# Batch 0's attention steps reordered by arrival of the data: keys' transposes ahead of q's, reciprocals split around the exponentials

## The chip, the cores and the metric

The kernel runs on one core of a Trainium2 chip. The metric is the device time of one launch in microseconds (us), lower is better. Two kernels are compared by runs in the same rounds on the same chip. A "look" below is the profiled execution of a kernel.

## The reference, cut to what matters

Attention with keys and values projected from 1024 positions to 64, then a two-layer network on the result. 8 batches, 8 heads, head size 64; the first product of the network is 512 to 2048 columns, the second 2048 to 512.

```python
def _attn_ref(q, k, v, E, F):
    k_proj = np.einsum('ks,bhsd->bhkd', E, k)
    v_proj = np.einsum('ks,bhsd->bhkd', F, v)
    scale = 1.0 / np.sqrt(q.shape[-1])
    scores = scale * np.matmul(q, k_proj.transpose(0, 1, 3, 2))
    scores = scores - np.max(scores, axis=-1, keepdims=True)
    attn = np.exp(scores)
    attn = attn / (np.sum(attn, axis=-1, keepdims=True) + 1e-09)
    return np.matmul(attn, v_proj)

def _moe_ref(x, w_in, w_out):
    h = x @ w_in
    g = h * np.clip(h + 3.0, 0.0, 6.0) / 6.0
    return g @ w_out
```

## The kernel before

The order on each engine is the order of the program (manual schedule). Batch 0 is loaded in pairs of heads, and its attention is worked pair by pair as the loads land; `busy(n)` puts n filler matmuls on constants into TensorE's stream, to keep its clock up while it would wait. All later batches are worked behind the products of the batch before them.

```python
def busy(n):
    ps = pmm()
    for _ in range(n):
        nc.tensor.matmul(ps, ones[:, :P], ones, start=True, stop=True)

for n, j in (("k", 0), ("q", 0), ("v", 0), ("k", 1), ("q", 1), ("k", 2), ("q", 2), ("v", 1),
             ("k", 3), ("q", 3), ("v", 2), ("v", 3)):
    nc.gpsimd.dma_start(out=kqv[0][n][:, 2 * j:2 * j + 2], in_=kqv_dram[n][0][:, 2 * j:2 * j + 2])
# ... w_in, batch 1 and w_out are loaded behind them
# ... E and F are transposed
busy(2)
```

```python
def by_pairs(self):                      # batch 0
    # keys(j): eight matmuls project the keys of pair j, VectorE copies them twice to kp
    # vals(j): the same for the values; the second copy may be later
    keys(0)
    self.q_out(0, self.q_transpose(0, pat))
    self.keys_transposed(0, 2)
    busy(2)
    self.scores(0, pmm)
    busy(3)
    vals(0)()
    keys(1)
    self.q_out(1, self.q_transpose(1, pat))
    lns = logs(0, both)
    self.keys_transposed(2, 2)
    busy(1)
    self.scores(1, pmm)
    recs = inverses(lns)
    av = self.values(0, pat, both)
    busy(3)
    keys(2)
    self.q_out(2, self.q_transpose(2, pat))
    lns = logs(1, one)
    self.keys_transposed(4, 2)
    busy(1)
    out(0, av, recs)
    self.scores(2, pmm)
    recs = inverses(lns)
    vals(1)()
    busy(3)
    keys(3)
    # ... pair 3: q in two halves, one copied by ScalarE; scores 3; values 2; sums 3
    rest.append(vals(3))
    busy(1)
    av = self.values(3, pat, one)
    out(3, av, recs)
    for copy in rest:
        copy()
    busy(4)
# ... then the first product, 16 groups of four matmuls; a group needs all four pairs:
h_ps = pmm()
for ko in range(KO):
    nc.tensor.matmul(h_ps, w_in_sb[:, ko, fo * P:(fo + 1) * P], xT[:, ko, t, :],
                     start=(ko == 0), stop=(ko == KO - 1))
```

The softmax here doesn't subtract the row's maximum and nothing guards it: scores larger than these inputs give would overflow.

## Time and profile before

| | |
|---|---|
| three runs before the prediction | 522.83 to 524.14 us, median 523.99 |
| profiled run | 522.67 us, span on the core 520.9 us |
| first matmul of the first product | 28.11 us |
| last load of batch 0 lands | 22.8 us |
| TensorE busy | 97% of the span |

The lines are shown in the prediction. In the view of the stretches, each row gives the length, then the busy time of each engine with its number of instructions, then the granted clock, the share of the transfer engines and GB/s. In a timeline a row begins with the start and the time to the last end of what it merges; the bracket says how long the engine was idle before and what ended that.

### The profile page before, as it was taken

What the parts mean: (1) busy time and instruction counts of PE and PEld (TensorE: products, weight loads), DVE (VectorE), ACT (ScalarE), POOL (GpSimd) and SP (SyncE); (2) the same over time, 40 slices, a digit from 0 to 9 for tenths busy, and PEclk for the clock granted to TensorE, in tenths of its full rate; (3) what the DMA queues carried; (4) which work ended last, traced back from release to release, by engine and by line L of the source; (5) the groups of instructions that cost most, each with busy time, mean ns of one, the idle gap of its engine ahead of it and who ended that gap; (6) DMA issues with size and microseconds to landing.
All of it is one profiled execution on the core that took longest, in us unless ns stands there. A gap on an engine that the chain in (4) does not pass through costs nothing.

```text
span 520.9 us, 7264 instructions
## 1 busy us (share of the span) xinstructions
PE 506.9 (97%) x2806; PEld 225.1 (43%) x2858; DVE 238.5 (46%) x378; ACT 283.9 (55%) x517; POOL 36.3 (7%) x55
## 2 busy tenths in 40 slices
PE   6899999999999999999999999999999999999996
PEld 3444444444444444444444444444444444444443
DVE  1568636444363453554454354534525544444420
ACT  2677485676446654568437664466635664444431
POOL 7620000100020000200002000200000000000000
PEclk9999999999999999999999999999999999999999
DMA  8999993993049711695119931298111110011112
GB/s 131 203 207 207 207 181 117 190 151 97 22 77 211 145 43 42 117 196 121 42 30 170 176 81 42 63 204 168 42 40 32 40 42 28 34 42 41 40 42 81
DMA packets 67443, 53.95 MB, mean 104 GB/s; under 512 B 29776, under 2 KB 59216, under 8 KB 67408
## 3 DMA queue, kind: packets, MB, share of 16 engines
q0 software_dynamic: 30016, 29.63, 35.6%
q1 hardware_dynamic: 37248, 23.73, 17.3%
q8 instruction: 22, 0.36, 0.3%
q10 hardware_dynamic: 144, 0.13, 0.1%
q14 instruction: 13, 0.11, 0.1%
HBM read 59.24 MB, written 16.78 MB: 146 GB/s over the span
## 4 chain that ended last, share of the span: by engine, by line
PE 94%; DMA 2%; issue 1%; DVE 1%; POOL 1%; ACT 1%; DVEq 0%; ACTq 0%; POOLq 0%
PE mm L393 43%; PE mm L402 41%; PE at L210 3%; PE at L150 3%; DMA q<-in_q_dram 2%; PE at L196 1%; PE mm L84 1%; PE at L180 1%; DVE qTp L187 0%; DVE xT L232 0%; DVE vp L162 0%; PE mm L210 0%; PE mm L196 0%; ACT aT L201 0%; POOL k L95 0%
## 5 line engine op out<-in xcount | busy, mean ns | idle before, releaser
L397 DVE SCALAR_TENSOR_TENSOR g<-r,mm 128x512 bf16<-128x512 f32 x256 | 173.4, 686 | 218.6 <-ACT r L396 218.4
L393 PE MATMUL mm<-xT,w_in_sb 128*128 128x512 bf16 x1000 | 233.1, 380 | 2.6 <-issue 1.9
L402 PE MATMUL mm<-w_out_sb,g 128*128 128x512 bf16 x999 | 230.1, 380 | 1.5 <-issue 0.3
L396 ACT ACTIVATE r<-mm 128x512 f32<-128x512 f32 x256 | 152.3, 603 | 62.6 <-PE mm L393 61.3
L393 PEld LDWEIGHTS <-w_in_sb 128*128 128x128 bf16 x1024 | 96.8, 98 | 125.6 <-issue 14.1
L402 PEld LDWEIGHTS <-g 128*128 128x128 bf16 x1024 | 98.9, 98 | 119.4 <-issue 2.2
L416 ACT COPY o_sb<-mm 128x512 f32<-128x512 f32 x63 | 36.9, 586 | 147.6 <-PE mm L402 144.7
L232 DVE TENSOR_TENSOR xT<-at,rec 128x512 bf16<-128x512 f32 x56 | 38.2, 684 | 16.5 <-ACT rec L228 15.4
L228 ACT ACTIVATE rec<-ln 128x512 f32<-128x512 f32 x64 | 40.4, 640 | 0.1
L223 ACT ACTIVATE ln<-at 128x512 f32<-128x512 f32 x59 | 32.7, 617 | 2.4 <-PE at L210 2.3
L201 ACT ACTIVATE aT<-at 128x512 bf16<-128x512 f32 x56 | 29.2, 612 | 0.9 <-PE at L196 0.9
L358 POOL COPY mark<-kT 1x1 bf16<-1x1 bf16 x5 | 0.9, 177 | 276.4 <-DMA kT<-kp 276.4
L150 PE MATMUL at<-k,ef_t 128*64 128x512 bf16 (+1 forms) x88 | 15.9, 323 | 1.1 <-DMA k<-in_k_dram 1.1
L150 PE MATMUL at<-v,ef_t 128*64 128x512 bf16 (+1 forms) x88 | 15.9, 324 | 0.0
L150 PEld LDWEIGHTS <-ef_t 128*64 128x64 bf16 x176 | 9.6, 109 | 11.4 <-issue 5.9
L162 DVE CAST vp<-at 64x512 bf16<-64x512 f32 (+1 forms) x21 | 11.3, 541 | 4.0 <-PE at L150 3.0
L210 PE MATMUL at<-aT,vp 64*64 64x512 bf16 x112 | 12.3, 379 | 0.5 <-DVE vp L162 0.4
L210 PE MATMUL at<-aT,ones 64*64 64x512 bf16 x118 | 12.7, 400 | 0.0
L84 PE MATMUL mm<-ones 128*128 128x512 bf16 x31 | 10.9, 446 | 1.6 <-DVE ones L77 1.5
L157 DVE CAST kp<-at 64x512 bf16<-64x512 f32 (+1 forms) x21 | 10.2, 522 | 4.3 <-PE at L150 4.3
L210 PEld LDWEIGHTS <-ones 64*64 64x64 bf16 x128 | 3.9, 103 | 13.4 <-issue 13.1
L196 PEld LDWEIGHTS <-kT 64*64 64x64 bf16 x256 | 5.8, 106 | 8.0 <-issue 5.1
(44 smaller groups left out, 94.8 us busy)
## 6 DMA issues: line engine op xcount, KB each, us to landing
out_dram<-o_sb SPq DMA_DIRECT2D x63, 256.0 KB, 2.0
q<-in_q_dram POOLq DMA_DIRECT2D x7, 1024.0 KB, 9.5
k<-in_k_dram POOLq DMA_DIRECT2D x7, 1024.0 KB, 15.0
v<-in_v_dram POOLq DMA_DIRECT2D x7, 1024.0 KB, 19.9
w_out_sb<-in_moe_w_out_dram POOLq DMA_DIRECT2D x4, 512.0 KB, 27.7
w_in_sb<-in_moe_w_in_dram POOLq DMA_DIRECT2D x3, 512.0 KB, 12.6
k<-in_k_dram POOLq DMA_DIRECT2D x4, 256.0 KB, 8.1
q<-in_q_dram POOLq DMA_DIRECT2D x4, 256.0 KB, 8.6
```

The costliest lines, as they stand in the source:

```text
L84: nc.tensor.matmul(ps, ones[:, :P], ones, start=True, stop=True)
L150: nc.tensor.matmul(ps[e * KP:(e + 1) * KP], ef_t[e][:, so, :], kqv[self.b]["kv"[e]][:, hs, so, :], start=(so == 0), stop=(so == SO - 1))
L201: nc.scalar.activation(self.aT[j][:, r].rearrange("p a n -> p (a n)"), tiles[r], AF.Exp, scale=scale)
L210: nc.tensor.matmul(tiles[t][c:c + D].rearrange("p (r n) -> p r n", r=2), stationary(r, 2 * j + a), self.aT[j][r:r + KP, :, a, :], start=Tr ...
L223: nc.scalar.activation(ln, den, AF.Ln)
L228: nc.scalar.activation(rec, ln, AF.Exp, scale=-1.0)
L232: nc.vector.tensor_mul(self.xT[:, j, t, :], av, rec)
L393: nc.tensor.matmul(h_ps, w_in_sb[:, ko, fo * P:(fo + 1) * P], xT[:, ko, t, :], start=(ko == 0), stop=(ko == KO - 1))
L396: nc.scalar.activation(r, h_ps, AF.Relu, bias=0.5, scale=1.0 / 6.0)
L397: nc.vector.scalar_tensor_tensor(g[:, fo, :], r, 1.0, h_ps, op0=ALU.min, op1=ALU.mult)
L402: nc.tensor.matmul(o_ps, g[:, fo, c * P:(c + 1) * P], w_out_sb[:, fo, :], start=(fo == 0), stop=(fo == FO - 1))
L416: nc.scalar.copy(o_sb, o_ps)
```

## The change

The intent is that each step stands where its data are there: the keys' transposes do not wait behind q's load, and a reciprocal (a log, then an exponential with scale -1) goes where ScalarE would be idle. The core of the diff:

```diff
             keys(0)
-            self.q_out(0, self.q_transpose(0, pat))
             self.keys_transposed(0, 2)
+            q_in_halves(0)                  # half copied by VectorE, half by ScalarE
             busy(2)
             self.scores(0, pmm)
-            busy(3)
+            busy(2)
 ...
             keys(1)
-            self.q_out(1, self.q_transpose(1, pat))
-            lns = logs(0, both)
+            den0 = self.sums(0, pmm)
+            ln0 = [self.log(den0[t]) for t in range(NB)]
+            rec0 = [self.inverse(ln0[0])]
             self.keys_transposed(2, 2)
-            busy(1)
+            self.q_out(1, self.q_transpose(1, pat))
+            busy(2)
             self.scores(1, pmm)
-            recs = inverses(lns)
+            rec0.append(self.inverse(ln0[1]))
 ...
             keys(2)
-            self.q_out(2, self.q_transpose(2, pat))
-            lns = logs(1, one)
+            busy(2)
             self.keys_transposed(4, 2)
+            self.q_out(2, self.q_transpose(2, pat))
+            ln1 = self.log(first(self.sums(1, pmm, one)))
             busy(1)
 ...                                        # pair 3: sums 3 ahead of values 2
             copy2(1)
             copy3(1)
-            busy(4)
+            busy(3)
```

More of the change, by code (lines that the diff above doesn't have):

```diff
@@ L236, in by_pairs, with pair @@
         def by_pairs(self):
-            both, one = (0, 1), (0,)
+            def pair(j):
+                return slice(2 * j, 2 * j + 2)
             def keys(j):
@@ L241, in keys @@
                 for so in range(SO):
-                    self.project(pk, 0, slice(2 * j, 2 * j + 2), so)
-                self.keys_out(pk, slice(2 * j, 2 * j + 2))
+                    self.project(pk, 0, pair(j), so)
+                self.keys_out(pk, pair(j))
             def vals(j):
@@ L247, in vals @@
                 for so in range(SO):
-                    self.project(pv, 1, slice(2 * j, 2 * j + 2), so)
-                self.values_out(pv, slice(2 * j, 2 * j + 2), copies=(0,))
-                return lambda: self.values_out(pv, slice(2 * j, 2 * j + 2), copies=(1,))
-            def logs(j, ts):
-                den = self.sums(j, pmm, ts)
-                return {t: self.log(den[t]) for t in ts}
-            def out(j, av, recs):
-                for t in recs:
-                    self.scaled(j, t, av[t], recs[t])
@@ L260, in inverses, with q_in_halves @@
-            def inverses(lns):
-                return {t: self.inverse(lns[t]) for t in lns}
+                    self.project(pv, 1, pair(j), so)
+                return lambda a: self.values_out(pv, pair(j), copies=(a,))
+            def q_in_halves(j):
+                self.qT[j] = att.tile([P, 2, TOK], bf16, tag="qTp", name="qTp")
+                halves = [self.q_transpose(j, pat, (a,)) for a in range(2)]
+                nc.vector.tensor_copy(self.qT[j][:, 0], halves[0])
+                nc.scalar.copy(self.qT[j][:, 1], halves[1])
@@ L263, in by_pairs, with first @@
+            def first(tiles):
+                return tiles[0]
+            one = (0,)
             keys(0)
-            self.q_out(0, self.q_transpose(0, pat))
             self.keys_transposed(0, 2)
+            q_in_halves(0)
             busy(2)
             self.scores(0, pmm)
-            busy(3)
-            vals(0)()
+            busy(2)
+            copy0 = vals(0)
+            copy0(0)
+            copy0(1)
             keys(1)
+            den0 = self.sums(0, pmm)
+            ln0 = [self.log(den0[t]) for t in range(NB)]
@@ L272, in by_pairs @@
+            rec0 = [self.inverse(ln0[0])]
+            self.keys_transposed(2, 2)
             self.q_out(1, self.q_transpose(1, pat))
-            lns = logs(0, both)
-            self.keys_transposed(2, 2)
-            busy(1)
-            self.scores(1, pmm)
-            recs = inverses(lns)
-            av = self.values(0, pat, both)
-            busy(3)
-            keys(2)
-            self.q_out(2, self.q_transpose(2, pat))
-            lns = logs(1, one)
-            self.keys_transposed(4, 2)
@@ L285, in by_pairs @@
-            busy(1)
-            out(0, av, recs)
-            self.scores(2, pmm)
-            recs = inverses(lns)
-            vals(1)()
-            busy(3)
+            busy(2)
+            self.scores(1, pmm)
+            rec0.append(self.inverse(ln0[1]))
+            av0 = self.values(0, pat)
+            self.scaled(0, 0, av0[0], rec0[0])
+            busy(2)
+            keys(2)
+            busy(2)
+            self.keys_transposed(4, 2)
+            self.q_out(2, self.q_transpose(2, pat))
@@ L292, in by_pairs @@
+            ln1 = self.log(first(self.sums(1, pmm, one)))
+            busy(1)
+            self.scores(2, pmm)
+            rec1 = self.inverse(ln1)
+            self.scaled(0, 1, av0[1], rec0[1])
+            copy1 = vals(1)
+            copy1(0)
+            copy1(1)
+            busy(2)
             keys(3)
-            lns = logs(2, one)
+            rec2 = self.inverse(self.log(first(self.sums(2, pmm, one))))
+            av1 = first(self.values(1, pat, one))
+            self.scaled(1, 0, av1, rec1)
@@ L294, in by_pairs @@
+            self.keys_transposed(6, 2)
             busy(2)
-            self.qT[3] = att.tile([P, 2, TOK], bf16, tag="qTp", name="qTp")
-            halves = [self.q_transpose(3, pat, (a,)) for a in range(2)]
-            self.keys_transposed(6, 2)
-            nc.vector.tensor_copy(self.qT[3][:, 0], halves[0])
-            nc.scalar.copy(self.qT[3][:, 1], halves[1])
-            av = self.values(1, pat, one)
-            out(1, av, recs)
+            q_in_halves(3)
             busy(2)
             self.scores(3, pmm)
-            recs = inverses(lns)
@@ L305, in by_pairs @@
             busy(2)
-            rest = [vals(2)]
-            av = self.values(2, pat, one)
-            out(2, av, recs)
-            recs = inverses(logs(3, one))
-            rest.append(vals(3))
-            busy(1)
-            av = self.values(3, pat, one)
-            out(3, av, recs)
-            for copy in rest:
-                copy()
-            busy(4)
+            copy2 = vals(2)
+            copy2(0)
+            rec3 = self.inverse(self.log(first(self.sums(3, pmm, one))))
+            av2 = first(self.values(2, pat, one))
@@ L319, in second_block @@
+            self.scaled(2, 0, av2, rec2)
+            copy3 = vals(3)
+            copy3(0)
+            busy(1)
+            av3 = first(self.values(3, pat, one))
+            self.scaled(3, 0, av3, rec3)
+            copy2(1)
+            copy3(1)
+            busy(3)
         def second_block(self):
```

## The prediction

> **What bounds the kernel now.** I read the page first (sections 1, 2 and 4), then the stretches, then the timelines of TensorE, VectorE and ScalarE up to 30 us.
>
> ```profile
> PE 506.9 (97%) x2806; PEld 225.1 (43%) x2858; DVE 238.5 (46%) x378; ACT 283.9 (55%) x517; POOL 36.3 (7%) x55
> ...
> PE   6899999999999999999999999999999999999996
> ...
> PE 94%; DMA 2%; issue 1%; DVE 1%; POOL 1%; ACT 1%; DVEq 0%; ACTq 0%; POOLq 0%
> ```
>
> TensorE is busy 97% of the span and is 94% of the chain that ended last. Only the first slices (13 us each) fall short, and the changed code lies there: batch 0's attention, up to the first matmul of the first big product (line 393 before).
>
> ```profile
> core 0: us, PE busy (x) PEld busy (x) DVE busy (x) ACT busy (x) POOL busy (x), PEclk, DMA share, GB/s
> 7.00:9.50 2.50, 0.79 (x12) 0.63 (x11) 0.48 (x2) 0.00 (x0) 2.35 (x4) 1.00 1.22 164
> 9.50:12.00 2.50, 2.28 (x24) 0.89 (x22) 0.82 (x2) 0.69 (x2) 1.13 (x2) 1.00 1.15 188
> 12.00:14.50 2.50, 1.83 (x29) 1.40 (x28) 1.06 (x4) 0.40 (x1) 1.35 (x3) 1.00 1.24 202
> 24.50:28.10 3.60, 3.08 (x26) 1.49 (x25) 1.96 (x4) 2.20 (x4) 1.44 (x2) 1.00 1.25 206
> ```
>
> Some 4 us of TensorE are idle between 5 and 28.1 us (18.8 us busy of 23.1), and part of the busy time is filler on constants. That is the ceiling of what any reorder here can win: below 1% of 524 us. Does a gain reach the end? After 28 us the waits of TensorE's matmuls are these:
>
> ```profile
> PE mm L393 <- issue: 1.9, 12, 0.2
> PE mm L402 <- issue: 0.3, 2, 0.2
> PE mm L210 <- DVE xT L232: 0.3, 1, 0.3
> ```
>
> No transfer is among them, so what moves the first product moves the end by the same amount. The timeline of TensorE at the end of batch 0's attention shows what sets that start:
>
> ```profile
> 25.32 0.40 PE L210 MATMUL at<-aT,vp 64*64 64x512 bf16 x2 [0.38 <-DVE vp L162]
> 25.55 0.38 PE L210 MATMUL mm<-aT,ones 64*64 64x512 bf16 x2
> 25.86 0.64 PE L150 MATMUL at<-v,ef_t 128*64 128x128 bf16 x8
> 26.43 0.39 PE L84 MATMUL mm<-ones 128*128 128x512 bf16 x1
> 26.90 0.40 PE L210 MATMUL at<-aT,vp 64*64 64x512 bf16 x2
> 27.24 1.04 PE L84 MATMUL mm<-ones 128*128 128x512 bf16 x3
> 28.11 3.62 PE L393 MATMUL mm<-xT,w_in_sb 128*128 128x512 bf16 x16
> ```
>
> The last load of batch 0 (v of pair 3) is issued at 12.86 us and lands 10.0 us later, at 22.8 us, yet its projection starts at 25.86. So at the end it is not the transfers that bound, but the hand-overs TensorE, VectorE, ScalarE and back. In this view the second number runs from the first start to the last end of a row; the next row's start gives the issue time, which I use below.
>
> **What the Trainium skill says.** (1) "TensorE: Matmul & The Clock Gate", Part 1, the HAM clock gate: after about 3.4 us idle the array drops to half clock. The stretch from 7 to 9.5 us is the emptiest (0.79 us busy) and its granted clock is 1.00; the reorder makes no longer hole, so I expect no drop. (2) "ScalarE: Activation LUTs", Table sets: exp and ln are in one set, so mixing reciprocals (ln, then exp) between the exponentials loads no table. The trace agrees: one table load, 1.28 us, at the start. (3) The same page, What ACT_TABLE_LOAD costs: 186 ns + 0.833 ns per column with immediates, 613 ns for 512; the trace has 600 (ln) to 630 (rec). Splitting a pair costs at most the overlap, about 0.1 us. (4) "VectorE: DVE Perf Modes", Why PSUM operands drop a tier: copies out of PSUM have at most two elements per cycle. The q copy of 1024 columns takes 692 ns, the half 414 ns: halving q between VectorE and ScalarE (585 ns) saves latency only when ScalarE is free.
>
> **The change part by part.** Nothing of the arithmetic changes. TensorE loses one filler matmul (24 to 23 in this stage; 0.22 us each). VectorE's copy of q for pair 0 is halved: VectorE gains back 0.28 us, ScalarE gets one more copy of 0.58 us while idle. For pairs 0 to 2 the keys' transposes come ahead of q's; the sums of pair 0 go ahead of q's transposes of pair 1; the logs and inverses are split around the exponentials; at the end the sums of pair 3 go ahead of the values of pair 2, and the last fillers go from four to three.
>
> I replayed the new order by hand with the durations of the old timelines. Issue times on TensorE: a projection of eight 0.57 us, eight transposes 0.55, two key transposes 0.16, eight scores 0.34, two or four sums or values 0.33, a filler 0.22. Results are ready 0.06 us (projection, transposes) to 0.07 us (the others) after that. VectorE: keys' two copies 0.48, kT 0.21, q 0.69 or 0.41, vp 0.30 each, xT 0.69. ScalarE: exponentials 1.09 a pair, logs 1.08 a pair, single ones 0.60 to 0.63. About 0.05 us for each hand-over. Loads land as before; the waits are those of the built program.
>
> Start in us, before (timeline) and after (replay):
>
> - keys 0: 7.20, 7.20 (k lands). kT of pair 0 ready: 10.80, 8.84.
> - q 0 transposed: 9.32, 9.32 (q lands). Its copies done: 10.67, then 10.15 on VectorE and 10.56 on ScalarE. Scores 0 ready: 11.27, 10.88. Exponentials 0 done: 12.40, 12.01.
> - values' projection 0: 11.95, 11.34. keys 1: 12.62, 12.62; it waits for k of pair 1 in both, and here the first gain (0.4 to 0.6 us) is lost.
> - sums 0: 14.44, 13.19. Logs 0 done: 15.97, 14.71. This is a gain of 1.3 us for ScalarE.
> - q 1 transposed: 13.89, 13.95 (lands 13.85). Then VectorE's q copy to 15.29, with kT already done: scores 1 start 15.43, 15.34. The keys' copy was only the last 0.14 us of that chain, so the gain here is 0.09 us.
> - one inverse is before the exponentials of pair 1: these run 15.88 to 16.97 before, 15.79 to 16.88 after.
> - keys 2: 16.74, 16.45. One filler fewer counts, the transfer (15.2) does not.
> - q 2 transposed: 17.31, 17.79. The data have been there since 16.4, but q now stands behind the keys' transposes, which wait for VectorE's keys copy (17.58). q copy done: 18.65, 19.13. Scores 2: 18.84, 19.18. **A loss of 0.34 us**: TensorE stands or runs fillers while q's transposes could run.
> - values' projection 1: 19.18, 19.52. keys 3: 20.50, 20.52 (one filler fewer wins 0.22 back, and the second filler row is gone from ahead of it).
> - sums 2, values 1, keys' transposes 3, q 3 in halves, scores 3: 23.41 before; after 23.32 for the first half and 23.63 for the second, which waits for ScalarE's half copy behind the inverse (22.77). Exponentials 3 done: 24.95, 25.03.
> - values' projection 2: 24.30, 24.23. sums 3: 25.55, 25.08. values 2: 25.32, 25.41. xT of pair 2: 25.83, 25.92. values 3: 26.90, 26.98, after VectorE's vp copy, which stands behind that xT.
> - fillers: 27.24 for four (0.87), 27.32 for three (0.65). First product: 28.11, **27.97**.
>
> The sum is 0.14 us earlier: -0.22 for the last filler, +0.08 for the rest, in which early gains are eaten by arrivals and by the wait in pair 2. The inverse of pair 3 (done 26.8) no longer bounds: its xT starts when the values are ready at 27.38 and ends 28.1, ahead of the fourth matmul at 28.6.
>
> 523.99 - 0.14 = 523.85. As the replay has many small waits rounded up, I say **523.7 us**.
>
> **The rivals.** (a) The early sums and logs carry through: ScalarE is 1.3 us ahead at pair 0, and if q's transposes in pair 2 overlapped better than I think, the end could come 0.5 to 1 us earlier: 523.0 to 523.5. For it: three us lie between the last landing and its use. Against it: pairs 2 and 3 are bound by VectorE's order (keys, kT, q, xT), not by ScalarE. (b) TensorE's order costs: each pair from 1 on puts q's transposes, 0.55 us, behind a wait for VectorE. If fillers do not hide it, 0.3 to 0.5 us more per pair: 524.3 to 525. For it: the replay of pair 2. Against it: pair 3's transposes stood behind fillers before as well. (c) The clock: fewer fillers and more holes could make the throttle drop for some 3 us, which at half speed costs 1.5 us or so: 525.5. Against it: 1.00 at 7 to 9.5 us with TensorE two thirds idle. (d) An earlier start collides with w_in or w_out. The first two w_in blocks land at 24.2 and 25.5, w_out at 51 to 58.6 and is first read at 59.7: 0.2 us do not matter.
>
> **Range and chances.** The replay's error I put at 0.5 us either way. The three runs before spread from 522.83 to 524.14, 1.3 us, more than the effect. Together: 522.4 to 525.0. A change of 2% is 10.5 us; the whole stage before the first product is 28 us with transfers until 22.8, so faster by 2% cannot come from here, and slower only from something broken.
>
> **What would show it.** Timeline after: kT of pair 0 copied by about 8.9; sums 0 at about 13.2; scores 1 near 15.3; q's transposes of pair 2 behind the keys' at about 17.8 and scores 2 near 19.2, later than before; the first product at 28.0, give or take 0.5; the span from there to the end equal within 0.5 us (492.8 us before: 520.9 less 28.1). I am wrong if the first product starts before 27.4 or after 28.6, if the granted clock drops below 1.00 after 7 us, or if the part after it changes by more than the noise.

## The result, and the profile after

| | before | changed |
|---|---|---|
| median of six runs | 523.81 us | 523.89 us |
| range | 521.88 to 524.15 | 521.76 to 524.65 |
| ratio (95% interval) | | 1.0004 (0.998 to 1.0028) |
| profiled span, its mean clock | 520.9 us, 0.999 | 522.4 us, 0.996 |
| first product starts | 28.11 | 29.58 |

A ratio is the mean time of one kernel's runs over the mean of the other's in the same rounds, so it is not quite the ratio of the medians. Executions over 1.5% slower than the fastest of the same kernel are left out of the means.

The time is the same, as predicted, but the profiled run did not look as predicted. Page and stretches of the changed kernel (the trace records the granted clock in steps of 3.41 us or a multiple; such a stretch is called a window below):

```profile
PE 512.8 (98%) x2857; PEld 226.0 (43%) x2857; DVE 238.7 (46%) x378; ACT 284.7 (55%) x518; POOL 36.3 (7%) x55
...
PEclk8999999999999999999999999999999999999999
```

```profile
6.58:9.99 3.41, 0.94 (x11) 0.66 (x10) 0.48 (x2) 0.56 (x1) 2.77 (x4) 1.00 1.16 168
9.99:13.40 3.41, 3.41 (x22) 1.31 (x21) 0.65 (x2) 1.43 (x3) 1.61 (x3) 0.50 1.20 189
```

From 9.99 to 13.40 us the granted clock was exactly one half. (The more numerous matmuls of this page say nothing of the change: this trace kept records that the earlier one lost.) The timeline of TensorE shows what came before that, and the end of the stage:

```profile
5.84 0.96 PE L84 MATMUL mm<-ones 128*128 128x512 bf16 x2
8.70 0.61 PE L150 MATMUL at<-k,ef_t 128*64 128x128 bf16 x8 [1.90 <-DMA k<-in_k_dram]
...
17.89 0.63 PE L150 MATMUL at<-k,ef_t 128*64 128x128 bf16 x8
...
20.67 0.41 PE L196 MATMUL mm<-qTp,kT 64*64 64x256 bf16 x8
...
28.59 0.40 PE L210 MATMUL at<-aT,vp 64*64 64x512 bf16 x2 [0.30 <-DVE vp L162]
28.92 0.82 PE L84 MATMUL mm<-ones 128*128 128x512 bf16 x3
29.58 3.62 PE L398 MATMUL mm<-xT,w_in_sb 128*128 128x512 bf16 x16
```

The very first keys landed 1.5 us later than in the profile before (8.66 against 7.16 us), TensorE waited 1.90 us for them, and a half clock followed. Neither was in my replay, so this profile alone cannot judge the order. Two things it does say. From the first product to the end it took 522.38 - 29.58 = 492.80 us; before, 520.90 - 28.11 = 492.79. What happens in this stage goes to the end one to one and nothing else changed. And from the start of keys 2 (17.89) to that of scores 2 (20.67) it took 2.78 us; before, 18.84 - 16.74 = 2.10:

```profile
16.74 0.63 PE L150 MATMUL at<-k,ef_t 128*64 128x128 bf16 x8
17.31 0.62 PE L180 MATMUL at<-ident,q 128*128 128x128 bf16 x8
...
18.19 0.23 PE L167 MATMUL at<-ident,kp 64*128 64x64 bf16 x2
...
18.84 0.41 PE L196 MATMUL mm<-qTp,kT 64*64 64x256 bf16 x8
```

### The profile page after: what moved, and what is told of

Read it like the earlier page. It is cut to its first block, busy times and chain, and to the rows that moved or that the text cites. A ratio compares the mean times of both kernels' runs of the same rounds, so it can differ in the third digit from the quotient of the medians.

```text
span 522.4 us, 7317 instructions
## 1 busy us (share of the span) xinstructions
PE 512.8 (98%) x2857; PEld 226.0 (43%) x2857; DVE 238.7 (46%) x378; ACT 284.7 (55%) x518; POOL 36.3 (7%) x55
## 4 chain that ended last, share of the span: by engine, by line
PE 95%; DVE 1%; DMA 1%; ACT 1%; issue 1%; POOL 0%; DVEq 0%; ACTq 0%; POOLq 0%
PE mm L398 43%; PE mm L407 41%; PE at L210 3%; PE at L150 3%; PE at L196 1%; DMA k<-in_k_dram 1%; PE mm L84 1%; PE at L180 1%; ACT aT L201 0%; PE mm L196 0%; PE mm L210 0%; DVE kp L157 0%; DVE qTp L187 0%; DVE xT L232 0%; DVE vp L162 0%
## 5 line engine op out<-in xcount | busy, mean ns | idle before, releaser
L398 PE MATMUL mm<-xT,w_in_sb 128*128 128x512 bf16 x1024 | 236.4, 379 | 0.0
L84 PE MATMUL mm<-ones 128*128 128x512 bf16 x33 | 12.5, 485 | 1.5 <-DVE ones L77 1.5
```

## The experiments

My theory after the result had three parts: the order's gain is lost at the landing of pair 1's keys and its loss lies in pair 2; the late load and the half clock are not the order's doing; and the end of the stage is bound by hand-overs and fillers that the change hardly touches. The main rival was that the new order brings the half clock, since it has fewer fillers and new waits.

**Run 1: the kernel before, unchanged, for its clocks.** No edit.

> The kernel before, unchanged, for the clock of each of its runs. Theory (holes): the runs of the changed kernel that took 523 us and more had a granted clock of 0.992 to 0.997, the one of 521.76 us had 1.000; in the profiled one the clock was half for 3.4 us from 9.99 us on, after TensorE had waited until 8.70 us for the first keys. If these drops come from the early wait and not from the new order, the runs of the kernel before show the same: clocks from 0.992 to 1.000, about 1.2 us longer per 0.003 of clock. Rival (new order): it brings the drops; then all runs of the kernel before are at 0.999 or 1.000 and near 522 us.

Measured: its six runs had clocks 1.0, 0.996, 0.992, 0.997, 1.0, 1.0 and times 521.83 to 524.01 us. The half clock comes without the new order too. Over all calls in which the clock of the kernel before is on record, by the mean clock of the run:

| | whole (0.998 to 1.000) | 0.995 to 0.997 | 0.990 to 0.993 |
|---|---|---|---|
| kernel before, 39 runs | 22 runs, mean 522.06 | 12, 523.02 | 5, 524.11 |
| changed kernel, 12 runs | 4 runs, mean 522.57 | 6, 523.44 | 2, 524.51 |

So most of the spread goes with the clock, not with the order: about 1 us for each loss of 0.003 to 0.004, which is what one window of 3.4 us at half clock takes from the mean (1.7 of 522 us). Whether the half clock itself or the late load that often comes with it costs this time, the table can't tell. In each column the changed kernel is 0.4 to 0.5 us longer, but not all from the same chip and with few runs; in the call of run 5 its two whole-clock runs have a mean of 522.45 us, those of the kernel before 522.24.

Whether 8 of 12 against 17 of 39 means a somewhat higher rate for the changed order stays open; with runs 6 to 8 below, which keep its start (8 of 18), it is 16 of 30, so it may be chance. Open, too, is the late first load: the first keys are issued at 2.41 or 2.42 us in all looks, but landed at 6.90 to 7.66 us in the four looks at the old order (before, runs 1, 2 and 11) and at 7.10 to 8.66 in the ten others, five of them above 8.2. No run tests why.

**Runs 2 and 3: both kernels with fillers where TensorE waits for the first loads.**

```diff
-    busy(2)                      # both kernels, ahead of the first keys
+    busy(10)
             keys(0)
+            busy(4)              # kernel before
             self.q_out(0, self.q_transpose(0, pat))
             keys(0)
+            busy(2)              # changed kernel
             self.keys_transposed(0, 2)
+            busy(2)
             q_in_halves(0)
```

> The kernel before with 8 more filler matmuls ahead of the first keys' projection and 4 between it and the first q transposes, where TensorE waits for loads. Theory (holes): granted clock 0.998 or more in every run, spread of the times below 1 us, mean about 1 to 1.5 us below the kernel before. If the fillers only delay: clock as before, time 0 to 1 us longer. First product in the profile at 28.1 to 28.5 us if the first keys land near 7.2 us.

> The changed kernel with 8 more fillers ahead of the first keys' projection and 2 + 2 around the first keys' transposes. Theory (holes): clock 0.998 or more in all runs, the profile free of the drop at 10 to 13 us, mean 1 to 1.5 us below the changed kernel as it is. Against the kernel before with the same fillers: the replay says the first product 0.14 us earlier (28.0 against 28.1) and the time the same within 0.5 us. If the changed order had a real gain of ScalarE's lead, its first product would be 0.5 us or more earlier than in the kernel before with fillers.

Measured: in no run was the clock halved at the start (two runs of run 2 have 0.998; the look at one of them shows the half clock from 519.85 us on, after TensorE's last matmul had ended at 517.59). The spread fell to 1.5 us and 1.2 us, not below 1. But the hoped-for 1 to 1.5 us did not come: 522.55 us median for the kernel before (ratio 1.0002), 523.15 for the changed one (1.0012), both against the kernel before. The fillers push the work back. In run 3 the ten of them began slow (0.43 us apart until 7.3 us, half of that later), and the first keys' projection started at 8.95 us although their load had landed at 7.21:

```profile
5.98 3.04 PE L84 MATMUL mm<-ones 128*128 128x512 bf16 x10
8.95 0.63 PE L150 MATMUL at<-k,ef_t 128*64 128x128 bf16 x8
```

So it is shown that filling the holes takes the half clock away (none of the 18 runs of runs 2 to 4), and this cure costs what it saves. Comparing the two orders by these looks is not fair, since the start of run 3 is late by the fillers alone; the later stretch can be compared: from keys 2 to the first product 11.37 us in run 2 and 11.69 in run 3, the same as in the profiles without fillers.

**Run 4: run 3 with the order in pair 2 turned back.**

```diff
-            busy(2)
-            self.keys_transposed(4, 2)
-            self.q_out(2, self.q_transpose(2, pat))
+            self.q_out(2, self.q_transpose(2, pat))
+            busy(2)
+            self.keys_transposed(4, 2)
```

> As the changed kernel with early fillers, but in pair 2 q's transposes and their copy come ahead of the keys' transposes, as in the kernel before. The replay: scores 2 come 0.34 to 0.45 us earlier after keys 2 (2.3 us after the start of keys 2 instead of 2.7), and the first product 0.3 us earlier than in the changed kernel with early fillers. Rival: the later part is bound by its own chain from scores 3 on and by fillers; then scores 2 come earlier but the first product stays within 0.1 us.

Measured: keys 2 at 17.25, scores 2 at 19.62, first product at 28.53 us: 2.37 and 11.28 us, each 0.41 less than in run 3. What is won in pair 2 goes to the first product whole. The time was 522.34 us (0.9999 of the kernel before; run 3 1.0012); with a whole start in all runs of both, the means are 522.39 and 523.11, the right direction and more than 0.41. The 2.37 us are still 0.27 more than in the kernel before: this edit leaves the two fillers of that place in, and their share was not tested.

**Run 5: the changed kernel once more, for a clean look.** No edit.

> The changed kernel, unchanged, for a look without a late first load and without the clock drop. In three looks at the kernel before (two of them unchanged, one with early fillers) the first product came 15.54 us after the landing of the keys of pair 1, whatever the start had been like. Replay: 15.40 us here if TensorE is waiting for that landing again; the stretch from keys 2 to the first product is 11.69 us as in the two looks so far, against 11.37 before. Rival (the new order is not pinned to the landing but to TensorE's own chain from the first keys on): the first product comes later than 15.6 us after that landing even with a clean start. Time within 0.5 us of the kernel before either way.

Measured: median 523.05 us against 523.03 of the kernel before, ratio 0.9999 (0.9982 to 1.0015). This profile has a whole clock, and the keys of pair 1 landed at 12.32:

```profile
12.37 0.63 PE L150 MATMUL at<-k,ef_t 128*64 128x128 bf16 x8 [0.39 <-DMA k<-in_k_dram]
...
16.24 0.63 PE L150 MATMUL at<-k,ef_t 128*64 128x128 bf16 x8
...
17.45 0.23 PE L167 MATMUL at<-ident,kp 64*128 64x64 bf16 x2
17.61 0.62 PE L180 MATMUL at<-ident,q 128*128 128x128 bf16 x8
...
19.01 0.41 PE L196 MATMUL mm<-qTp,kT 64*64 64x256 bf16 x8
...
27.27 0.82 PE L84 MATMUL mm<-ones 128*128 128x512 bf16 x3
27.92 3.40 PE L398 MATMUL mm<-xT,w_in_sb 128*128 128x512 bf16 x15
```

TensorE waits 0.39 us for pair 1's keys, so all that was won before is lost there. From that landing to the first product it is 27.92 - 12.32 = 15.60 us: the replay said 15.40, the kernel before has 15.54. The 15.60 us lie on the rival's line; the wait of 0.39 us rules it out for a clean start. For a late start (the look of the result, run 3) it holds: there TensorE comes late to those keys.

This look also hints at what the half clock hangs on. Its first keys landed at 7.84 us and TensorE waited 1.75 us for them, hardly less than the 1.90 us in the look of the result. But the windows lie elsewhere: here 4.99 to 8.41 us, with TensorE busy 1.67 us in it; there 6.58 to 9.99, with 0.94. The first window with a whole clock begins anywhere from 4.25 to 7.48 us in the 14 looks.

**Run 6: the changed kernel with pair 2 turned back, no early fillers.** The edit of run 4 on the changed kernel.

> The changed kernel with only the order in pair 2 turned back (q's transposes ahead of the keys'), without early fillers. From the look with early fillers: keys 2 to scores 2 in 2.37 us (2.78 in the changed kernel), keys 2 to first product 11.28 us (11.69). So 0.4 us less time than the changed kernel as it is, if the start is the same. If the gain was given back by something else in that look, 11.6 us or more.

Measured: keys 2 at 17.81, scores 2 at 20.18, first product 29.09: 2.37 and 11.28 us as expected. The median, 523.65 us (1.0005), does not show the 0.4 us: four of its six runs, the profiled one too, had a halved clock. Its two runs with a whole clock were 522.10 and 522.25 us. The stretch is a clear result, the time an inconclusive one.

**Run 7: the later part in order of readiness, without fillers at the end.** Built on run 6, shortened; a line with # stands for calls that are left out or only move:

```diff
             copy1(1)
-            busy(2)
             keys(3)
-            # log 2, inverse 2, values 1, multiplication 1, keys' transposes 3
-            busy(2)
             q_in_halves(3)
-            busy(2)
+            ln2 = self.log(first(self.sums(2, pmm, one)))
+            self.keys_transposed(6, 2)
+            av1 = first(self.values(1, pat, one))
+            busy(1)
             self.scores(3, pmm)
-            busy(2)
+            self.scaled(1, 0, av1, rec1)
+            rec2 = self.inverse(ln2)
             copy2 = vals(2)
             copy2(0)
-            # log 3, inverse 3, values 2, multiplication 2
+            copy2(1)
             copy3 = vals(3)
             copy3(0)
-            busy(1)
+            # values 2, multiplication 2, sums 3, log 3, inverse 3
             # values 3, multiplication 3
-            copy2(1)
             copy3(1)
-            busy(3)
```

> As the one before, and from pair 1's values on in an order by readiness: q 3 right behind keys 3, its half copy on ScalarE ahead of the log, values' projections 2 and 3 behind scores 3 (under the exponentials), values 2 ahead of sums 3, no fillers at the end. Theory (the end of the stage is bound by the hand-overs behind scores 3 and by fillers, not by loads): scores 3 some 1 us earlier; exponentials, sums, log, inverse and one multiplication follow, so the first product starts at about 25.5 and its fourth matmul waits for the last multiplication at about 27: the time 2 us below the kernel before. Rival (the last loads bind): the first product cannot start before 27.5, the time is the same within 0.7 us.

Measured: 520.34 us median, ratio 0.9954 (0.9936 to 0.9973). In its timeline both projections of values lie under the exponentials (the row of 16), and the fourth matmul waits:

```profile
22.90 0.41 PE L196 MATMUL mm<-qTp,kT 64*64 64x256 bf16 x8
23.25 1.08 PE L150 MATMUL at<-v,ef_t 128*64 128x128 bf16 x16
24.26 0.40 PE L210 MATMUL at<-aT,vp 64*64 64x512 bf16 x2
24.50 0.40 PE L210 MATMUL mm<-aT,ones 64*64 64x512 bf16 x2
24.91 0.40 PE L210 MATMUL at<-aT,vp 64*64 64x512 bf16 x2
25.25 0.87 PE L394 MATMUL mm<-xT,w_in_sb 128*128 128x512 bf16 x3
26.97 2.97 PE L394 MATMUL mm<-xT,w_in_sb 128*128 128x512 bf16 x13 [0.85 <-DVE xT L232]
```

This look had a late first load and a halved clock, keys 2 only at 17.56, and still the first product began at 25.25. The last loads do not bind in either kernel; the hand-overs and fillers do. This run changes the order and takes out 11 of 23 fillers at once (2.4 us of TensorE at 0.22 each), so what each is worth is not shown.

**Run 8: three groups ahead.** The first three groups begin with the nine matmuls that need pairs 0 to 2 only (shortened):

```diff
+            if fo == 0:
+                held.extend(pmm() for _ in range(ahead))      # ahead = 3
+                for ko in range(KO - 1):
+                    for f in range(ahead):
+                        by_ko(held[f], xT, t, f, (ko,))
+            h_ps = held[fo]
+            by_ko(h_ps, xT, t, fo, range(KO - 1, KO))
```

> As the one before, and the first three groups of the first product begin with the nine matmuls that do not need the last pair. Theory: they fill the wait of the fourth matmul, about 1 us; the time 2.5 to 3 us below the kernel before (0.5 to 0.6%), the clearest of all runs. Rival: VectorE and ScalarE, which then get three groups at once, make TensorE wait for free PSUM tiles afterwards; then less than 0.3 us better than the run before.

Measured: 519.92 us median, ratio 0.9941 (0.9924 to 0.9957). By whole-clock runs alone: 519.70 (4 runs) against 520.24 (4 runs) of run 7. The step is worth some 0.5 us, between theory (1) and rival (below 0.3). In its look the wait of 0.85 us is gone, though the clock had been half for two windows (6.8 us).

**Runs 9 and 10: run 8 with four more fillers at the start.**

```diff
-    busy(2)
+    busy(6)                      # run 9
-    busy(2)
+    busy(4)                      # run 10
             keys(0)
+            busy(2)              # run 10
             self.keys_transposed(0, 2)
```

> The fast tail with groups, and six fillers instead of two ahead of the first keys. In ten looks the half clock followed a window of 3.41 us in which TensorE was busy 0.94, 1.03, 1.26 and 1.26 us, and never one of 1.67 us or more. Four fillers add 0.9 us (1.7 us at half clock). Theory: no half clock in any run, mean 0.5 us below the same kernel with two fillers (which had it in some of its runs), spread under 1 us. Rival: they push the first keys back by as much as they save, so the mean is the same within 0.2 us.

> As the run before, with the four extra fillers placed two ahead of the first keys and two between the first keys' projection and their transposes, where TensorE waits 0.58 us for VectorE anyway. Theory: no half clock, and less push-back than six in one row; mean the same or 0.2 us lower than with six.

Measured: run 9 had a whole clock in five of five runs, 519.53 to 520.32 us, median 519.73, ratio 0.9951 (0.9937 to 0.9966). Run 10 had clocks of 0.995 and 0.990 in two of its six: 519.17 to 523.53 us, median 519.63, ratio 0.9967 (0.994 to 0.9993). Of the means, run 9 has 519.83 us and run 8 had 520.00, but on another chip, and the ratios (0.9951 and 0.9941) say the reverse: whether the rival's "same within 0.2" holds stays open. What run 9 shows is a steady time. Run 10 refutes my "no half clock". The look at run 9 shows the next bound:

```profile
20.69 0.62 PE L180 MATMUL at<-ident,q 128*128 128x128 bf16 x8 [0.90 <-DMA q<-in_q_dram]
...
24.96 0.38 PE L395 MATMUL mm<-xT,w_in_sb 128*128 128x512 bf16 x1 [0.16 <-PE at L210]
25.59 3.20 PE L395 MATMUL mm<-xT,w_in_sb 128*128 128x512 bf16 x14 [0.25 <-DMA w_in_sb<-in_moe_w_in_dram]
```

TensorE waits 0.90 us for q of pair 3 and 0.25 us for the third group's weights, which land at 25.5 us. Now loads bind, so the order of this stage has little left to win.

**Run 11: the kernel before with the order of pair 2 alone changed.**

```diff
-            self.q_out(2, self.q_transpose(2, pat))
-            lns = logs(1, one)
             self.keys_transposed(4, 2)
+            self.q_out(2, self.q_transpose(2, pat))
+            lns = logs(1, one)
```

> The kernel before with one part of the change alone: in pair 2 the keys' transposes ahead of q's. The replay's step: keys 2 to scores 2 takes 2.10 us in three looks at the kernel before; here the transposes wait for the keys' copy, so 2.6 to 2.8 us, and the first product comes 0.4 to 0.6 us later after keys 2 (11.37 us before). If the order in pair 2 did not matter there: 2.1 us and 11.4 us.

Measured (one look, 523.22 us, clock 0.996):

```profile
16.62 0.63 PE L150 MATMUL at<-k,ef_t 128*64 128x128 bf16 x8
17.82 0.23 PE L167 MATMUL at<-ident,kp 64*128 64x64 bf16 x2 [0.57 <-DVE kp L157]
17.99 0.62 PE L180 MATMUL at<-ident,q 128*128 128x128 bf16 x8
...
19.39 0.41 PE L196 MATMUL mm<-qTp,kT 64*64 64x256 bf16 x8
...
28.66 2.54 PE L393 MATMUL mm<-xT,w_in_sb 128*128 128x512 bf16 x11
```

Keys 2 to scores 2 takes 2.77 us instead of 2.10, and the first product comes 12.04 us after keys 2 instead of 11.37: 0.67 us both times, a little above what I expected. TensorE stands 0.57 us for VectorE's copy of the keys with q's data at hand. The half clock came here too, in the old order, after a window in which TensorE was busy 1.44 of 3.41 us.

**Run 12: the changed kernel with pair 0 as before.**

```diff
-            self.keys_transposed(0, 2)
-            q_in_halves(0)
+            self.q_out(0, self.q_transpose(0, pat))
+            self.keys_transposed(0, 2)
```

> The changed kernel with pair 0 as before (q transposed first and copied whole by VectorE). The replay's claim: the 0.4 us won there are lost again at the landing of the keys of pair 1. So the first product comes 15.6 us after that landing as in the clean look at the changed kernel (15.60), if TensorE reaches it in time and the clock is whole. If pair 0's gain does carry, 15.9 to 16.0 us.

Measured (one look, 523.83 us): inconclusive. The clock was half from 11.08 us on, the projection of values 0 began at 12.66, after the keys of pair 1 had landed (12.12), and the first product came 29.25 - 12.12 = 17.1 us after them. The condition of the test was not met. That pair 0's gain is lost at the landing rests on the wait of 0.39 us in run 5, not on this run.

## Why the prediction was right, and where it was not

**The time.** Predicted 523.7 us and the same within 2%; measured 523.89, and 1.0004 and 0.9999 in two sets of rounds. The range held. That the number came within 0.2 us is luck: the median of the kernel before alone went from 522.04 to 523.99 us.

**The sum, step by step, in the clean look.** The change of the first product relative to the landing of pair 1's keys:

| step | before | replay | measured (run 5) |
|---|---|---|---|
| landing of pair 1's keys to keys 2 | 4.17 | 3.88 | 3.92 |
| keys 2 to scores 2 | 2.10 | 2.73 | 2.77 |
| scores 2 to first product | 9.27 | 8.79 | 8.91 |
| sum | 15.54 | 15.40 | 15.60 |

The mechanism was right: a gain of 0.25 us ahead of keys 2, a loss of 0.67 us in pair 2, and 0.36 us won behind it, where the stage has 12 fillers instead of 14 (that they are the cause was not tested alone). Each term came out within 0.12 us, yet together they turned the predicted gain of 0.14 us into a loss of 0.06. The largest miss is the last term. Within it scores 3 to the values' projection 2 took 1.08 us (24.32 - 23.24) where I had 0.91, because the second half of the scores waits for ScalarE's copy and the fillers behind it start later too. My habit of then rounding the replay's 523.85 down to 523.7 went the wrong way; the replay needed rounding up. Two readings of the prediction were incomplete, without effect on its sum: in pair 3, too, the keys' transposes now come ahead of q's, and the last slice of TensorE falls short as well as the first ones.

**That it goes to the end** was right: 492.79 us before, 492.80 in the look of the result, 520.70 - 27.92 = 492.78 in run 5.

**The step that failed is rival (c), the clock.** I wrote that the reorder makes no longer hole and that I expect no drop, with the clock of 1.00 at 7 to 9.5 us as the argument, and gave "the granted clock drops below 1.00 after 7 us" and a first product after 28.6 us as signs of being wrong. Both signs appeared in the profiled run, and the prediction of the time held all the same: the drop comes in the kernel before as well (17 of 39 runs), so it cancels in the comparison as far as the rates are alike. What failed in the argument: 7 to 9.5 us was a stretch of my choosing. The windows of that profile were 4.79 to 8.20 and 8.20 to 11.61 us, with TensorE busy 1.92 and 2.07 us; in the look of the result one had 0.94, and the half clock followed. I had one profile of a random thing and took it for the rule. It even stood in the three times before: 522.83 to 524.14 us is wider than the steps of this stage can explain.

**Rival (a)**, ScalarE's lead carries through: not seen. Sums 0 did come early (12.93 us in run 5, 14.44 before), and none of it is seen at the end. **Rival (b)**, the order costs: right for pair 2 by 0.67 us (run 11), made up elsewhere. I had not weighed that the order and the fillers behind pair 2 were the larger reserve: runs 7 and 8 won 2.4 and 3.1 us there. (Half a per cent, but with intervals clear of 1.)

## What to carry to other kernels

A step belongs where its data are there: moving a transpose whose input was ready behind one that waits for VectorE cost 0.67 us, while moves ahead of a pending load won nothing. Before tuning a start-up stage by single profiles, look at the clock and times of some dozen runs: runs with a halved clock took 1 to 2 us longer in the mean, more than any step of this change. And count the fillers: the three behind the last wait moved the first product by 27.92 - 27.27 = 0.65 us in run 5. Not all of that comes back when they go: in run 7, without them, the fourth matmul waited 0.85 us.

## What the Trainium skill lacked or had wrong

- "TensorE: Matmul & The Clock Gate", Part 1 and the table of "Why this matters for your kernels": the page has the clock halve after an idle window of about 3.4 us and asks for no idle gaps over some 3 us. (A section of it, "A second HAM failure mode", has the clock also fall after frequent short idles, without a figure for how much.) Its window length agrees (half clock from 9.99 to 13.40 us, 3.41 us). But no idle window is needed: the clock was halved after windows of 3.41 us in which TensorE was busy 0.94, 1.03, 1.26, 1.26, 1.44 and 1.59 us (the look of the result, runs 6, 7, 8, 11, 12), the longest single wait in the first of them being 1.90 us. It stayed whole after 1.67, 1.74, 1.92 us and more (runs 5, 1, the kernel before; up to 3.38 in run 4). The windows at the end of the 14 looks fit: half clock after 1.39 us (run 4) and less, whole after 1.78 us (run 8) and more. So in these looks the line lies between 47 and 49% busy.
- The same page, Part 1, says that the clock comes back after a busy window. In run 8 a window of half clock with 2.59 us busy was followed by another at half clock; after 3.41 us (the look of the result) and 3.33 us (run 11) it came back. The page gives no share.
